# A gated attention and token-mixer kernel: o visits in twos and ones, and one ring of six banks for s and ms

## The chip, the cores and the metric

The kernel runs on one core of a Trainium2 chip. The time is the device time of the program in microseconds (us). Before the change it was 1692.79 us, the median of three runs (1692.36 to 1693.18). A profile of one further execution shows what each engine does: PE is TensorE's matmuls, PEld its weight loads, DVE VectorE, ACT ScalarE, POOL GpSimd, and SP the queue that issues the DMAs.

## The reference

With S = 2048 rows, D = 640 columns, H = 32 query heads of 20 columns, one key head and one value head, and F = 1728:

```python
g = sigmoid((x * gate_w).sum(-1, keepdims=True))
q = heads(A_x @ A_wq)                      # 32 heads of 20
k, v = A_x @ A_wk, A_x @ A_wv              # one head each
p = softmax(q k^T * 20 ** -0.5)
a = join(p @ v) @ A_wo
h = layernorm(B_x)
u = gelu(h^T @ B_w1 + B_b1)                # along the rows
b = (u @ B_w2 + B_b2)^T
out = g * a + (1 - g) * b
```

All inputs are fp32. The kernel splits operands in a high and a low part (`_hi`, `_lo`) and adds three products (high by high, low by high, high by low), so most matmuls come in threes.

## The kernel before

An opening part projects q, k and v, writes q to memory (`q_scr`), and computes a first share of the mixer. Then comes the loop that this case is about.

**Units.** Attention is cut in 32 groups of (four heads by 512 query columns), and each group in 16 blocks of 128 keys: 512 units `(n, kb)` in all. A unit has these steps:

- `qk` (L642): four matmuls named s, one for each head, on half of TensorE's rows (head half `b`, rows 0 to 63 or 64 to 127). An s fills one PSUM bank of 512 columns. ScalarE's exp (L652) turns it to a tile p in SBUF.
- `pv_mm` (L670): the o visit. Four heads' p by v, on four column tiles of 32, added up over the 16 units of a group in one bank o. At the group's last unit o is read by VectorE (transpose L685), scaled, transposed back (L692), split and stored to `o_scr`; these steps stand in `later` and are taken one or two at a time by `settle` (L972).
- `ms_next` (L454): the maxima that the softmax subtracts. An ms is a matmul of 128 queries by 512 keys on one row half, and VectorE's reduce (L469) reads it. 64 of them make a group's maxima. `ms_done` (L476) reduces them to `mm` (L480, VectorE) and makes `mn` of it in three GpSimd operations (L482 to L484). `store_max` (L487) transposes `mn` on VectorE (L490) and stores it, at the visit of unit 7 of the group before; `fetch_max` (L493), at that of unit 9, loads the maxima as extra rows of q.

**Fillers.** The rest of TensorE's work in the loop is cut in matmuls of 64 rows by 320 columns that all add into one bank, g: the remaining 18 tiles of the mixer's first product (`b1_jobs`, 96 fillers each), its second product (`b2_jobs`, 32 parts of 81), and a part of the output projection (`a_job`, 30 fillers for 128 rows by 320 columns). When fillers pass from one row half to the other, `signal` (L660) puts a small VectorE operation (`flag`) between them.

**The loop.** 488 stretches, each followed by one visit. In stretch `k`, row half `b = k % 2` has four s and three or four ms (`lane_x`), the other half has some ten fillers and one ms or none (`lane_f`); `beside` (L947) writes the two lanes in one order by the estimates `X_US` and `F_US`. Half `b` makes its s of units `k - 1` and `k`. Then follows the visit of unit `k - 1`. In `batches` (L903) a part of the first product is cut in 5 x 2 stretches and one of the second in 4 x 2; a part of the output projection takes 3 (`a_job`).

**The tail.** The last 24 visits have no ms left. `stretch` (L1011) makes one visit once, and then two at a time, over s and the rest of the output projection (`tail_job`, `tail_take`). A closing part adds the last four heads and stores eight pieces.

**Banks.** Of eight PSUM banks, three are `ps_m` (ms), three `ps_s` (s), one g and one o. Tiles p rotate through 12 buffers.

**What the output projection loads.** `load_o` and `load_y` bring o and y back for a tile; `wo2` and the last two columns of `oTs` hold copies of two chunks at the other row half, so that a part's fillers can be parted unevenly between the halves.

Of the kernel before, what the change touches and what calls it, by code (L numbers as in the profile page):

```python
# [17 lines left out]
P = 128  # L18
# [6 lines left out]
NB = 512  # L25
# [5 lines left out]
TAIL = 24  # L31
EPS = 1e-5
# [5 lines left out]
def mix_kernel(ctx: ExitStack, tc: tile.TileContext, A_x, A_wq, A_wk, A_wv, A_wo,  # L38
# [411 lines left out]
    mtiles = {}  # L450
    given = [0, 0]
    issued = [0, 0]

    def ms_next(b):  # L454
# [7 lines left out]
        def step():  # L462
            if n not in mtiles:
                mtiles[n] = mpool.tile([P, 16, 4], F32, name="mp")
            ms = ps_m.tile([P, NB], F32, name="ms")
            nc.tensor.matmul(ms, qmax[n][64 * b:64 * b + 60, pr, qt * P:(qt + 1) * P],  # L466
                             kst[64 * b:64 * b + 60, kq * NB:(kq + 1) * NB], start=True, stop=True)
            c = (2 * b + pr) * 4 + qt
            nc.vector.tensor_reduce(mtiles[n][:, c, kq:kq + 1], ms, axis=AX.X, op=ALU.max)  # L469
            issued[b] += 1  # L470
            if min(issued) == 32 * n + 1:
                new_qmax(n + 1)
# [82 lines left out]
    with tc.tile_pool(name="psb", bufs=2, space=PSUM, side="right") as psb:  # L555
# [8 lines left out]
        for fc in range(PRO):  # L564
# [32 lines left out]
    OC = DC + 2  # L597
    oTs = [slot[1][:, 2 * DC * D + i * 2 * OC * P:2 * DC * D + (i + 1) * 2 * OC * P]
           .rearrange("p (j c q) -> p j c q", j=2, q=P) for i in range(2)]
    twin = ctx.enter_context(tc.tile_pool(name="twin", bufs=1))  # L600
    wo2 = [twin.tile([P, 2, HD2], F32R, name=name) for name in ("wo2_hi", "wo2_lo")]
    yts = []
    pools = {}

    def second():
        right.close()
        ys = ctx.enter_context(tc.tile_pool(name="ys", bufs=1, side="right"))
        yts.extend(ys.tile([P, D], F32, name=f"y{i}") for i in range(2))
        pools["rows"] = ctx.enter_context(tc.tile_pool(name="rows", bufs=3, side="right"))
# [12 lines left out]
    def load_wo2():  # L622
        wos[DC] = fin.tile([P, D], F32, name="yo")
        for d in range(2):
            o = 64 * (1 - d)
            nc.sync.dma_start(out=wos[DC][o:o + 64, :].rearrange("p (c e) -> p c e", c=2),
                              in_=A_wo[:2 * P, d * HD2:(d + 1) * HD2].rearrange("(c h p) e -> h p c e", c=2, h=2)[d])

    def split_wo2():
        wr = wos[DC].rearrange("p (c e) -> p c e", c=2)  # L630
        nc.gpsimd.tensor_copy(wo2[0], wr)
        nc.gpsimd.tensor_sub(wo2[1], wr, f32(wo2[0]))

# [6 lines left out]
    odd_s = [0]  # L640

    def qk(u, pr, b):  # L642
# [4 lines left out]
        odd_s[0] ^= 1  # L647
        s = ps_m.tile([P, NB], F32, name="ms") if spare[0] and odd_s[0] and not loaded else ps_s.tile([P, NB], F32, name="s")
        nc.tensor.matmul(s, kst[64 * b:64 * b + 62, kb * P:(kb + 1) * P], q[64 * b:64 * b + 62, pr, :],  # L649
                         start=True, stop=True)  # L650
        p = pp_pool.tile([P, NB], F32, name="p")
# [89 lines left out]
    def load_o(st):  # L741
        cols = slice(st * P, (st + 1) * P)
        for j in range(2):
            oT = f32(oTs[st % 2][:, j])
            nc.sync.dma_start(out=oT[:, :DC], in_=o_scr[j, :, cols].rearrange("(c p) s -> p c s", p=P))
            for h in range(2):
                nc.sync.dma_start(out=oT[64 * (1 - h):64 * (2 - h), DC:],
                                  in_=o_scr[j, :2 * P, cols].rearrange("(c h p) s -> h p c s", c=2, h=2)[h])

    def load_y(st):  # L750
        nc.sync.dma_start(out=yts[st % 2], in_=y_scr[st * P:(st + 1) * P, :])
# [6 lines left out]
    NA = NS - 7  # L758
    jobs = [(st, 0, D) for st in range(NS - 8, NS - 4)]
# [3 lines left out]
    def room(i):  # L763
        t, at = (u0, 3 * D * i) if i < 4 else (slot[0], 3 * D * (i % 4))
# [55 lines left out]
    def a_job(st, d):  # L820
        hold = {}
        sl = slice(d * HD2, (d + 1) * HD2)
        last_one = st == NA - 1

        def mm(c, k, half):
            if not hold:
                hold["p"], hold["n"] = ps_g.tile([P, NB], F32, name="g"), 0
            hold["n"] += 1
            r = slice(64 * half, 64 * half + 64)
            o = oTs[st % 2][r, k % 2, c, :]  # L830
            w = (wo_lo if k == 2 else wo_hi)[r, c, sl] if c < DC else wo2[k // 2][r, c - DC, :]
            other_tile(half, nc.tensor.matmul(hold["p"][:, :HD2], o, w,  # L832
                                              start=(hold["n"] == 1), stop=(hold["n"] == 6 * DC)))

        def done():
            if d == 0:
                rows_a[st] = fin.tile([P, D], F32, name="yo")
            at = rows_a[st]
            nc.scalar.activation(at[:, sl], hold["p"][:, :HD2], AF.Copy, scale=g_col[:, st:st + 1])
            nc.gpsimd.tensor_add(at[:, sl], at[:, sl], yts[st % 2][:, sl])  # L840
            if d == 1 or last_one:
# [3 lines left out]
        def steps(half, cks):  # L845
            return [lambda c=c, k=k: mm(c, k, half) for c, k in cks]

        every = [(c, k) for c in range(OC) for k in range(3)]
        if last_one:
            own = every[:3 * DC]  # L850
            fs = [steps(1, own[:8]), steps(0, own[:8]), steps(1, own[8:]), steps(0, own[8:])]
        else:
            most, few = every[:-1], every[5:3 * DC]
            fs = [steps(1 - d, most[:10]), steps(d, few), steps(1 - d, most[10:])]
        out = [(f, [], []) for f in fs]
        out[-1][2].append(done)
        if d == 0 and not last_one:
            out[0][1].extend((lambda: load_o(st + 1), lambda: load_y(st + 1)))
        return out

    rows_a = {}
# [55 lines left out]
    k_tail = len(units) - TAIL  # L917
    todo = [divmod(i, FC) for i in range(PRO, 2 * FC)]
    seq = batches([b1_jobs(*t) for t in todo], [5] * len(todo))
    for i, (steps, rest, done) in enumerate(seq):  # L920
        item, j = divmod(i + 1, 5)
        rest.insert(0, lambda c=4 * (PRO + item) + (48 * j // 5) // 12: w1_upto(c + 4))
    b2 = [b2_jobs(st) for st in range(NS)]
    m = len(seq)
    seq += batches(b2, [4] * 2 * NS)
    for st in range(NS - 1):
        for j, n in ((1, 1), (2, 2), (3, 4)):
            seq[m + 8 * st + 4 + j][1].append(lambda c=W2 + 4 * (st + 1) + n: w1_upto(c))
# [4 lines left out]
    seq[m + 9 + 8 * DC][1].append(load_wo2)  # L933
    seq[m + 11 + 8 * DC][1].append(split_wo2)
    seq[-8][1].append(lambda: load_o(0))
    seq[-1][1].append(lambda: load_y(0))
    ph = [(rows[1 - b], rest if b else [], done if b else []) for rows, rest, done in seq for b in range(2)]
    for st in range(NA):
        for d in range(2 if st < NA - 1 else 1):
            ph += a_job(st, d)  # L940
    assert len(ph) == k_tail
    for i, k in enumerate((443, 451, 459, 467, 473, 477, 481, 485)):
        ph[k][1].append(lambda i=i: tail_load(i))

    X_US, F_US = 0.232, 0.147

    def beside(rows0, rows64, x):  # L947
        lanes = [list(rows0), list(rows64)]
        at = [0.0, 0.0]
        while lanes[0] or lanes[1]:  # L950
            k = 0 if lanes[0] and (not lanes[1] or at[0] <= at[1]) else 1
            if k == x and len(lanes[k]) == 1 and lanes[1 - k]:
                k = 1 - k
            us, f = lanes[k].pop(0)
            f()
            at[k] += us

    def lane_x(ss, ms):
        out = []
        for x in ss:  # L960
            out += [(X_US, y) for y in ms[:1]] + [(X_US, x)]
            ms = ms[1:]
        return out + [(X_US, y) for y in ms]

    def lane_f(ms, fs, end):
        return [(F_US, f) for f in fs] + [(0.0, f) for f in [signal] + end] + [(X_US, y) for y in ms]
# [5 lines left out]
    def settle(k):  # L972
# [14 lines left out]
    for k in range(k_tail):  # L987
        b = k % 2
        ss = [lambda u=u, pr=pr: qk(u, pr, b) for u in (k - 1, k) for pr in range(2) if u >= 0]
        fs, rest, done = ph[k]  # L990
        ms = [[f for f in (ms_next(x) for _ in range(c)) if f] for x, c in (((b, 3), (1 - b, 1)) if len(fs) < 12 else ((b, 4), (1 - b, 0)))]
        lanes = [None, None]
        lanes[b] = lane_x(ss, ms[0])
        lanes[1 - b] = lane_f(ms[1], fs, done)
        if k == 0:
            (m0, m1, m2), (s0, s1) = ms[0], ss
            lanes[0] = [(3 * X_US, m0), (3 * X_US, m1), (X_US, s0), (X_US, m2), (X_US, s1)]
        beside(*lanes, b)
# [5 lines left out]
        if k == k_tail - 4:  # L1004
            raw = last_wo()
        if k == k_tail - 2:
            w_last = split_last(raw)
        if k:
            visit(k - 1)

    def stretch(k, n):  # L1011
        lanes = [None, None]
        for b in range(2):
            own = [j for j in range(k, k + n) if j % 2 == b]
            ss = [lambda u=u, pr=pr, b=b: qk(u, pr, b) for j in own for u in (j - 1, j) for pr in range(2) if u < len(units)]
            fs = tail_take(b, math.ceil(len(tail[b]) * n / (len(units) + 1 - k)) + (n == 1) * (3 if not ss else -3))
            cut = [0] + [round(len(fs) * x) for x in ((0.25, 0.5, 0.75, 1.0) if n == 1 else
                                                          (0.18, 0.53, 0.82, 1.0) if b == k % 2 else (0.41, 0.71, 1.0, 1.0))]
# [67 lines left out]
```

## Time and profile before

| | us |
|---|---|
| median of three runs | 1692.79 |
| the profiled execution, its own time | 1692.96 |
| its span, from the first to the last instruction | 1691.2 |

The granted TensorE clock is 1.000 over the whole span. The page gives busy times as unions over each engine, so a lane beside another is not counted twice. A row of a group names its line, engine, operation, tiles and shapes, its count, its busy time, the mean length of one in ns, and the idle time ahead of it with what ended it. In rows in order of time the first number is the start and the second how long the merged instructions took; a matmul's length contains its passage through the array, so its neighbour in the same lane starts earlier than it ends.

### The profile page before, as it was taken

How to read it: one execution, taken by the hardware profiler on the slowest of the kernel's cores; microseconds unless marked ns; L12 is line 12 of the kernel's file. 1: busy time of each engine (PE TensorE's matmuls, PEld its weight loads, DVE VectorE, ACT ScalarE, POOL GpSimd, SP SyncE). 2: the span in 40 equal slices, each digit the busy share in tenths (PEclk: the TensorE clock that was granted, in tenths of full speed). 3: DMA queues.
4: the chain of work that ended last, by engine and by line, in shares of the span. 5: the costliest groups of instructions: out<-in, count | busy, mean ns of one | idle time of the engine just before them, and what ended most of it. 6: DMA issues, size and time to landing. Idle time of an engine off the chain costs nothing.

```text
span 1691.2 us, 39115 instructions
## 1 busy us (share of the span) xinstructions
PE 1683.8 (100%) x14865; PEld 1100.5 (65%) x14865; DVE 1433.7 (85%) x2913; ACT 1186.7 (70%) x2323; POOL 574.0 (34%) x726
## 2 busy tenths in 40 slices
PE   9999999999999999999999999999999999999998
PEld 7899766666666666666666666666666666666666
DVE  6679888888888888888888888888888888888834
ACT  4444677777777777777777777777777777777775
POOL 6467644543545454322222222222211122111200
PEclk9999999999999999999999999999999999999999
DMA  7665322222222222112122222121112222455511
GB/s 209 196 178 148 95 64 64 65 64 68 59 71 71 71 64 70 54 54 55 44 70 70 68 71 63 57 61 52 50 36 63 62 60 66 103 159 157 153 57 50
DMA packets 180450, 139.13 MB, mean 82 GB/s; under 512 B 33402, under 2 KB 146455, under 8 KB 180263
## 3 DMA queue, kind: packets, MB, share of 16 engines
q1 hardware_dynamic: 180262, 136.63, 29.2%
q8 instruction: 117, 1.92, 0.5%
q14 instruction: 71, 0.57, 0.1%
HBM read 103.94 MB, written 31.65 MB: 80 GB/s over the span
## 4 chain that ended last, share of the span: by engine, by line
PE 96%; issue 2%; DVE 1%; DMA 0%; ACT 0%; POOL 0%; SPq 0%; POOLq 0%; DVEq 0%; ACTq 0%
PE o L676 30%; PE s L649 18%; PE ms L466 17%; PE g L721 12%; PE g L894 8%; PE pu L576 4%; PE pp L293 4%; PE g L832 2%; PE ms L794 1%; PE pt L285 0%; PE pp L357 0%; DMA xb<-in_A_x_dram 0%; DVE mp L469 0%; PE g L794 0%; PE pp L182 0%
## 5 line engine op out<-in xcount | busy, mean ns | idle before, releaser
L469 DVE TENSOR_REDUCE mp<-ms 128x1 f32<-128x512 f32 x2048 | 1278.5, 684 | 166.6 <-PE ms L466 160.5
L652 ACT ACTIVATE p<-s 128x512 f32<-128x512 f32 x2048 | 1067.1, 604 | 393.8 <-PE s L649 389.2
L466 PE MATMUL ms<-kst,qmx 60*128 60x512 f32 x2048 | 848.5, 419 | 0.5 <-DVE mp L469 0.4
L649 PE MATMUL s<-qst,kst 62*128 62x512 f32 x2048 | 744.3, 404 | 0.0
L676 PE MATMUL o<-p,v_sb 128*32 128x512 f32 x4096 | 555.3, 604 | 0.0
L466 PEld LDWEIGHTS ms<-kst,qmx 60*128 60x128 f32 x2048 | 378.3, 185 | 207.3 <-DVE flag L662 181.1
L649 PEld LDWEIGHTS s<-qst,kst 62*128 62x128 f32 x2048 | 379.0, 186 | 13.3 <-issue 10.9
L894 PE MATMUL g<-slot,wh 64*128 64x320 f32 x1152 | 281.4, 318 | 0.0
L124 POOL TENSOR_TENSOR wl<-wr,wh 128x512 fp32r<-128x512 f32 (+1 forms) x176 | 220.5, 1255 | 35.1 <-ACT wh L121 22.6
L123 POOL CAST wh<-wr 128x512 fp32r<-128x512 f32 (+1 forms) x136 | 79.8, 587 | 443.1 <-PE g L721 280.0
L894 PEld LDWEIGHTS g<-slot,wh 64*128 64x128 f32 x1152 | 190.6, 184 | 59.9 <-DVE flag L662 59.9
L721 PE MATMUL g<-u,wh 64*128 64x320 f32 x864 | 208.8, 317 | 0.0
L721 PE MATMUL g<-slot,wh 64*128 64x320 f32 x864 | 208.8, 317 | 0.0
L676 PEld LDWEIGHTS o<-p,v_sb 128*32 128x32 f32 x4096 | 94.2, 108 | 137.6 <-issue 130.3
L894 PE MATMUL g<-slot,wl 64*128 64x320 f32 x576 | 179.4, 311 | 0.0
L721 PEld LDWEIGHTS g<-slot,wh 64*128 64x128 f32 x864 | 142.4, 184 | 40.2 <-DVE flag L662 40.2
L721 PEld LDWEIGHTS g<-u,wh 64*128 64x128 f32 x864 | 142.4, 184 | 40.2 <-DVE flag L662 40.2
L721 PE MATMUL g<-slot,wl 64*128 64x320 f32 x432 | 135.1, 313 | 0.0
L721 PE MATMUL g<-u,wl 64*128 64x320 f32 x432 | 134.9, 313 | 0.0
L894 PEld LDWEIGHTS g<-slot,wl 64*128 64x128 f32 x576 | 106.1, 184 | 15.1 <-DVE flag L662 15.1
L721 PEld LDWEIGHTS g<-slot,wl 64*128 64x128 f32 x432 | 79.6, 184 | 13.4 <-DVE flag L662 13.4
L721 PEld LDWEIGHTS g<-u,wl 64*128 64x128 f32 x432 | 79.5, 184 | 13.4 <-DVE flag L662 13.4
(201 smaller groups left out, 1417.8 us busy)
## 6 DMA issues: line engine op xcount, KB each, us to landing
wr<-in_B_w_dram SPq DMA_DIRECT2D x152, 256.0 KB
qmx<-q_scr SPq DMA_DIRECT2D x192, 80.0 KB
qst<-q_scr SPq DMA_DIRECT2D x192, 80.0 KB
slot<-o_scr SPq DMA_DIRECT2D x18, 320.0 KB
y_scr<-yo SPq DMA_DIRECT2D x16, 320.0 KB
o_scr<-oh SPq DMA_DIRECT2D x124, 40.0 KB
o_scr<-ol SPq DMA_DIRECT2D x124, 40.0 KB
q_scr<-qh SPq DMA_DIRECT2D x19, 256.0 KB
```

The source lines that it names most:

```text
L123: nc.gpsimd.tensor_copy(wh, wr)
L124: nc.gpsimd.tensor_sub(wl, wr, f32(wh))
L293: nc.tensor.matmul(pp, w, t, start=first and n == 0, stop=not more and n == len(steps) - 1)
L466: nc.tensor.matmul(ms, qmax[n][64 * b:64 * b + 60, pr, qt * P:(qt + 1) * P], kst[64 * b:64 * b + 60, kq * NB:(kq + 1) * NB], start=True, s ...
L469: nc.vector.tensor_reduce(mtiles[n][:, c, kq:kq + 1], ms, axis=AX.X, op=ALU.max)
L576: nc.tensor.matmul(pu[r][:, :HD2], w[rows, c, :], h[rows, st, :], start=(st == 0 and k == 0), stop=(st == NS - 1 and k == 2))
L649: nc.tensor.matmul(s, kst[64 * b:64 * b + 62, kb * P:(kb + 1) * P], q[64 * b:64 * b + 62, pr, :], start=True, stop=True)
L652: nc.scalar.activation(p, s, AF.Exp, scale=SCALE)
L676: nc.tensor.matmul(o[32 * hh:32 * hh + 32, :], v_sb[:, kb, :], ptiles.pop((u, hh)), start=(kb == 0), stop=(kb == NS - 1), skip_group_check ...
L721: other_tile(half, nc.tensor.matmul(hold["p"][:, :HD2], w[r, fc % HS, :], u[d][r, fc, :], start=(hold["n"] == 1), stop=(hold["n"] == 6 * F ...
L832: other_tile(half, nc.tensor.matmul(hold["p"][:, :HD2], o, w, start=(hold["n"] == 1), stop=(hold["n"] == 6 * DC)))
L894: other_tile(half, nc.tensor.matmul(hold["p"][:, :HD2], w[r, st % HS, :], h[d][r, st, :], start=(hold["n"] == 1), stop=(hold["n"] == 6 * NS)))
```

## The change

- The loop goes over 326 stretches: none, two, one, two, one ... visits behind them. Parts of the first product are cut in 3 x 2 stretches (16 fillers each), of the second in 3 x 2 (13 or 14), of the output projection in 2 (15).
- A stretch has six s on half `b`. With 16 fillers it has five ms there and one on the other half; with fewer, five and two before two visits, four and one before one visit. The orders are written out in `MANY` and `FEW`, and `merged` lays the lanes side by side. The s are no longer tied to `k`: `s_next` gives each half its next s.
- Where two visits stand together and the first is the last of its group, it goes to the middle of the stretch.
- `next_bank` takes `ps_m` and `ps_s` in turn for s and ms alike. Two more p buffers are used once the maxima are done.
- The tail has blocks of three and two visits (`BLOCKS`).
- The output projection in the loop ends at half of tile 6 instead of half of tile 8; the tail has the more. The copies `wo2` and the two further columns of `oTs` go.
- At the end, the stores are issued after the computation, six on SP's queue and two on ScalarE's.

```diff
+BLOCKS = (3, 3, 2, 3, 3, 3, 3, 2, 2)
...
+    ring = []
+
+    def next_bank():
+        if not ring:
+            return ps_m.tile([P, NB], F32, name="ms")
+        ring[0] ^= 1
+        return ps_m.tile([P, NB], F32, name="ms") if ring[0] else ps_s.tile([P, NB], F32, name="s")
...
-            ms = ps_m.tile([P, NB], F32, name="ms")
+            ms = next_bank()
...
+    def next_p():
+        turn_p[0] += spare[0]
+        i = turn_p[0] % 14
+        return extra_p[i - 1] if 0 < i < 3 else pp_pool.tile([P, NB], F32, name="p")
+
+    def s_next(b):
+        j = sc[b]
+        if j >= 2 * len(units):
+            return None
+        sc[b] += 1
+        return lambda: qk(j // 2, j % 2, b)
...
-        s = ps_m.tile([P, NB], F32, name="ms") if spare[0] and odd_s[0] and not loaded else ps_s.tile([P, NB], F32, name="s")
+        s = ps_s.tile([P, NB], F32, name="s") if spare[0] else next_bank()
...
-    NA = NS - 7
-    jobs = [(st, 0, D) for st in range(NS - 8, NS - 4)]
+    NA = NS - 9
+    jobs = [(st, 0, D) for st in range(NA - 1, NS - 4)]
...
-    seq = batches([b1_jobs(*t) for t in todo], [5] * len(todo))
+    seq = batches([b1_jobs(*t) for t in todo], [3] * len(todo))
...
-    seq += batches(b2, [4] * 2 * NS)
+    seq += batches(b2, [3] * 2 * NS)
...
+    seq += batches(aj, [1] * (2 * NA - 1))
...
-    for k in range(k_tail):
-        b = k % 2
-        ss = [lambda u=u, pr=pr: qk(u, pr, b) for u in (k - 1, k) for pr in range(2) if u >= 0]
+    FEW = (("smsssmssmmm", "mFm"), ("smsmsmssms", "Fm"))
+    MANY = (("msmsmsssmsm", "Fm"), ("msmsmsssmsm", "Fm"))
+
+    def main(k, vs):
+        b = k % 2
         fs, rest, done = ph[k]
...
+            sx, sf = (MANY if len(fs) > 15 else FEW)[len(vs) == 1]
+            lx = [(X_US, (s_next if c == "s" else ms_next)(b)) for c in sx]
+            lf = []
+            for c in sf:
+                lf += fill if c == "F" else [(X_US, (s_next if c == "s" else ms_next)(1 - b))]
+        order = merged(lx, lf)
+        for i, f in enumerate(order):
+            if len(vs) == 2 and 2 * i >= len(order):
+                settle()
+                if units[vs[0]][1] == NS - 1:
+                    visit(vs[0])
+                vs = vs[1:] if units[vs[0]][1] == NS - 1 else vs + [None]
+            f()
         ms_done()
         spare[0] = len(row_max) == NU
-        settle(k)
+        settle()
         for f in rest:
             f()
...
+        for v in vs:
+            if v is not None:
+                visit(v)
...
+    for k in range(len(ph)):
+        n = 0 if k == 0 else 1 + k % 2
+        main(k, list(range(v, v + n)))
+        v += n
...
+    for n in BLOCKS:
+        ends = [min(2 * len(units), 2 * (v + n) + (1 if n == 3 else 2)) for _ in range(2)]
...
+        for _ in range(n):
+            settle()
+            visit(v)
+            v += 1
...
-            nc.sync.dma_start(out=y_out[st * P:(st + 1) * P, sl], in_=at[:, :HD2])
+            ends[i, d] = at
+    for q, order in ((nc.sync, ((0, 0), (1, 0), (0, 1), (2, 1), (1, 1), (2, 0))), (nc.scalar, ((3, 0), (3, 1)))):
+        for i, d in order:
+            st = NS - 4 + i
+            q.dma_start(out=y_out[st * P:(st + 1) * P, d * HD2:(d + 1) * HD2], in_=ends[i, d][:, :HD2])
```

More of the change, by code (lines that the diff above doesn't have):

```diff
@@ L596, in mix_kernel @@
     wo_hi, wo_lo = (slot[1][:, i * DC * D:(i + 1) * DC * D].rearrange("p (c d) -> p c d", d=D) for i in range(2))
[L597 to L603, printed above, removed]
+    oTs = [slot[1][:, 2 * DC * D + i * 2 * D:2 * DC * D + (i + 1) * 2 * D].rearrange("p (j c q) -> p j c q", j=2, q=P)
+           for i in range(2)]
+    yts = [f32(slot[1][:, 2 * DC * D + 4 * D + i * D:2 * DC * D + 4 * D + (i + 1) * D]) for i in range(2)]
+    pools, extra_p = {}, []
     def second():
         right.close()
-        ys = ctx.enter_context(tc.tile_pool(name="ys", bufs=1, side="right"))
-        yts.extend(ys.tile([P, D], F32, name=f"y{i}") for i in range(2))
+        xp = ctx.enter_context(tc.tile_pool(name="xp", bufs=1, side="right"))
+        extra_p.extend(xp.tile([P, NB], F32, name=f"p{i}") for i in range(2))
         pools["rows"] = ctx.enter_context(tc.tile_pool(name="rows", bufs=3, side="right"))
@@ L620, in split_wo @@
         nc.gpsimd.tensor_sub(wo_lo[:, c, :], wr, f32(wo_hi[:, c, :]))
[L622 to L632, printed above, removed]
     units = [(n, kb) for n in range(NU) for kb in range(NS)]
@@ L818, in tail_take, with a_jobs, load, mm @@
         return out
-    def a_job(st, d):
+    def a_jobs(st):
         hold = {}
[L822 to L826, printed above, removed]
+        ds = (0,) if st == NA - 1 else (0, 1)
+        def load():
+            oT, yt = oTs[st % 2], yts[st % 2]
+            load_a(st, D, oT, yt)
+            hold["o"], hold["y"] = oT, yt
+        total = 6 * DC
+        def mm(c, k, d, half):
+            if not hold.get("n"):
                 hold["p"], hold["n"] = ps_g.tile([P, NB], F32, name="g"), 0
+            oT = hold["o"]
+            o, w = ((oT[:, 0], wo_hi), (oT[:, 1], wo_hi), (oT[:, 0], wo_lo))[k]
@@ L828, in mm @@
             hold["n"] += 1
             r = slice(64 * half, 64 * half + 64)
[L830 to L835, printed above, removed]
-            if d == 0:
[L837 to L841, printed above, removed]
+            other_tile(half, nc.tensor.matmul(hold["p"][:, :HD2], o[r, c, :], w[r, c, d * HD2:(d + 1) * HD2],
+                             start=(hold["n"] == 1), stop=(hold["n"] == total)))
@@ new lines, in done @@
+        def done(d):
+            sl = slice(d * HD2, (d + 1) * HD2)
+            if d == 0:
+                hold["a"] = fin.tile([P, D], F32, name="yo")
+            at, yt = hold["a"], hold["y"]
+            hold["n"] = 0
+            if spare[0]:
+                nc.vector.scalar_tensor_tensor(at[:, sl], hold["p"][:, :HD2], g_col[:, st:st + 1], yt[:, sl],
+                                               op0=ALU.mult, op1=ALU.add)
+            else:
+                nc.scalar.activation(at[:, sl], hold["p"][:, :HD2], AF.Copy, scale=g_col[:, st:st + 1])
+                nc.gpsimd.tensor_add(at[:, sl], at[:, sl], yt[:, sl])
+            if d == ds[-1]:
@@ L842, in done @@
                 e = slice(0, (d + 1) * HD2)
                 nc.sync.dma_start(out=y_out[st * P:(st + 1) * P, e], in_=at[:, e])
[L845 to L861, printed above, removed]
+        return load, [([[lambda h=h, c=c, k=k, d=d: mm(c, k, d, h) for h in range(2)]
+                        for c in range(DC) for k in range(3)],
+                       lambda d=d: done(d)) for d in ds]
     def spare_row(i, dt=F32):
@@ L1007, in mix_kernel @@
             w_last = split_last(raw)
[L1008 to L1018, printed above, removed]
-            lanes[b] = [x for i in range(4) for x in [(X_US, y) for y in ss[i:i + 1]] +
-                        [(F_US, f) for f in fs[cut[i]:cut[i + 1]]]]
-        beside(*lanes, None)
-        for j in range(k, k + n):
-            settle(j)
-            if 13 <= j - k_tail < 17:
-                tail_load(8 + j - k_tail - 13)
-            visit(j - 1)
@@ L1028, in mix_kernel @@
-    stretch(k_tail, 1)
-    for k in range(k_tail + 1, len(units), 2):
-        stretch(k, 2)
+    assert v == len(units) - TAIL and spare[0]
+    for n in BLOCKS:
+        ends = [min(2 * len(units), 2 * (v + n) + (1 if n == 3 else 2)) for _ in range(2)]
+        lanes = [[], []]
+        own = [(2 * len(units) - c) * X_US for c in sc]
+        i = 0
+        while any(sc[b] < ends[b] for b in range(2)):
+            b = int(sc[1] < sc[0])
+            lanes[b].append((max(0.0, 0.55 + (i - 2) * EXP_US) if i > 2 else 0.0, s_next(b)))
+            i += 1
+        left = len(units) - v
+        fs = [tail_take(b, len(tail[b]) if n == left else
+                        max(0, round(((own[b] + len(tail[b]) * F_US) * n / left - len(lanes[b]) * X_US) / F_US)))
+              for b in range(2)]
+        at = [0.0, 0.0]
+        while any(lanes) or any(fs):
+            b = 0 if at[0] <= at[1] and (lanes[0] or fs[0]) or not (lanes[1] or fs[1]) else 1
+            if lanes[b] and (lanes[b][0][0] <= at[b] or not fs[b]):
+                lanes[b].pop(0)[1]()
+                at[b] += X_US
+            else:
+                fs[b].pop(0)()
+                at[b] += F_US
+        for _ in range(n):
+            settle()
+            visit(v)
+            v += 1
+        waiting = {j for h in range(2) for j, _ in tail[h]}
+        while len(loaded) < len(jobs) and len(loaded) - 8 not in waiting and (len(loaded) < 10 or v >= 501):
+            tail_load(len(loaded))
@@ L1047, in mix_kernel @@
     oh, ol = osplit
+    ends = {}
     for i in range(4):
```

91 lines of the change are left out of this document (37 added, 54 removed).

## The prediction

> **What bounds the kernel now.** I read the page first (busy times, chain of waits, costliest groups), then busy time by stage, then the order of time on the engines. The page's shares:
>
> ```profile
> span 1691.2 us, 39115 instructions
> ...
> PE 1683.8 (100%) x14865; PEld 1100.5 (65%) x14865; DVE 1433.7 (85%) x2913; ACT 1186.7 (70%) x2323; POOL 574.0 (34%) x726
> ...
> PE 96%; issue 2%; DVE 1%; DMA 0%; ACT 0%; POOL 0%; SPq 0%; POOLq 0%; DVEq 0%; ACTq 0%
> PE o L676 30%; PE s L649 18%; PE ms L466 17%; PE g L721 12%; PE g L894 8%; PE pu L576 4%; PE pp L293 4%; PE g L832 2%; PE ms L794 1%; PE pt L285 0%; PE pp L357 0%; DMA xb<-in_A_x_dram 0%; DVE mp L469 0%; PE g L794 0%; PE pp L182 0%
> ...
> L469 DVE TENSOR_REDUCE mp<-ms 128x1 f32<-128x512 f32 x2048 | 1278.5, 684 | 166.6 <-PE ms L466 160.5
> L652 ACT ACTIVATE p<-s 128x512 f32<-128x512 f32 x2048 | 1067.1, 604 | 393.8 <-PE s L649 389.2
> ```
>
> TensorE is the chain, and nothing it waits for is large. VectorE is next at 85%. Busy time by stage (first fillers, second fillers, output fillers, tail, end; columns are stretch and length, then PE, PEld, DVE, ACT, POOL):
>
> ```profile
> 179.50:703.00 523.50, 523.39 (x4596) 326.62 (x4597) 466.04 (x953) 390.56 (x771) 245.50 (x321) 1.00 0.25 67
> 703.00:1455.50 752.50, 752.50 (x6692) 469.47 (x6692) 665.87 (x1361) 546.97 (x1060) 175.64 (x236) 1.00 0.21 58
> 1455.50:1607.70 152.20, 152.20 (x1346) 94.35 (x1342) 134.95 (x277) 114.65 (x226) 29.35 (x39) 1.00 0.60 161
> 1607.70:1678.60 70.90, 70.90 (x697) 45.68 (x695) 23.84 (x47) 50.81 (x101) 3.43 (x6) 1.00 0.14 41
> ```
>
> The loop's 180 + 256 + 52 stretches take 2.908, 2.939 and 2.927 us, 1428.2 in all. Inside one, TensorE in order of time:
>
> ```profile
> 1004.91 0.40 PE L466 MATMUL ms<-kst,qmx 60*128 60x512 f32 x1
> 1005.23 1.06 PE L676 MATMUL o<-p,v_sb 128*32 128x512 f32 x8
> 1006.23 0.42 PE L721 MATMUL g<-u,wh 64*128 64x320 f32 x1
> 1006.23 0.50 PE L466 MATMUL ms<-kst,qmx 60*128 60x512 f32 x1
> 1006.49 0.31 PE L721 MATMUL g<-u,wh 64*128 64x320 f32 x1
> 1006.57 0.39 PE L649 MATMUL s<-qst,kst 62*128 62x512 f32 x1
> ...
> 1007.74 0.47 PE L649 MATMUL s<-qst,kst 62*128 62x512 f32 x1
> 1007.81 0.30 PE L721 MATMUL g<-u,wl 64*128 64x320 f32 x1
> ```
>
> Two lanes run side by side. An s or ms follows another after 0.234 (five steps from 1006.57 to 1007.74), a filler after 0.147 (nine steps from 1006.49 to 1007.81). The first step after a visit is longer: 0.34 and 0.26. From the last start to the visit is 0.32; from visit to the next row start 1.00. The tail already has two visits in a row:
>
> ```profile
> 1615.49 1.92 PE L676 MATMUL o<-p,v_sb 128*32 128x512 f32 x16
> 1617.35 0.50 PE L649 MATMUL s<-qst,kst 62*128 62x512 f32 x2
> ```
>
> That is 1.86, so the second costs 0.86. One turn from row tiles to column tiles and back therefore costs (0.34 - 0.234) + (0.32 - 0.234) + (1.00 - 0.86) = 0.33 us.
>
> My formula for a stretch is: last start of the longer lane, + 0.32, + the visit. Seven entries end at 0.34 + 5 x 0.234 = 1.51; 9.6 fillers, then ms, at 0.26 + 8.6 x 0.147 = 1.52. Stage one gets 2.84 (measured 2.908); stage two, with 10.1 fillers, 2.92 (2.939). I add 0.04 a stretch.
>
> **The change: fewer turns.** 488 stretches become 326, with the same matmuls in them and in the tail. Pairs of stretches (two visits, one visit):
>
> - Stage one, 54 pairs, eleven entries against sixteen fillers and an ms: 0.34 + 9 x 0.234 = 2.45 and 0.26 + 15 x 0.147 = 2.465. Pair: 2 x (2.465 + 0.32 + 0.04) + 1.00 + 1.86 = 8.51; total 459.5.
> - Stage two, 96 pairs, some 13.5 fillers. One visit: ten entries, 2.21, with 0.36 behind them 2.57. Two visits: eleven entries, 2.45 without waits.
> - Output stage, 13 pairs, 15 fillers. One visit: 0.26 + 14 x 0.147 = 2.32, so 2.68. Two visits: at most 2.54 in the filler lane.
>
> **The ring.** Six banks alternate whatever they hold, so each allocation waits for the one six before it. The rows that price it:
>
> ```profile
> 1003.34 0.49 PE L466 MATMUL ms<-kst,qmx 60*128 60x512 f32 x1
> 1003.67 0.39 PE L649 MATMUL s<-qst,kst 62*128 62x512 f32 x1
> 1003.87 2.50 DVE L469 TENSOR_REDUCE mp<-ms 128x1 f32<-128x512 f32 x4 [0.44 <-PE ms L466]
> 1004.10 2.06 ACT L652 ACTIVATE p<-s 128x512 f32<-128x512 f32 x4 [0.81 <-PE s L649]
> ...
> 602.64 1.25 DVE L469 TENSOR_REDUCE mp<-ms 128x1 f32<-128x512 f32 x2
> 603.35 0.49 PE L466 MATMUL ms<-kst,qmx 60*128 60x512 f32 x1
> ```
>
> A reduce starts 0.53 after a first ms, then each 0.605 ((2.50 - 0.684) / 3). An exp starts 0.43 after its s (0.54 after a first one, whose matmul is 0.11 longer), then each 0.485. A bank is taken again 0.03 after the reader's mean end (602.64 + 0.684 to 603.35); I use 0.05.
>
> Stage one, order m s m s m s s s m s m m: the tenth taker needs the second s's bank (0.77 + 0.485 + 0.65 = 1.91, wanted at 2.21), the eleventh the third reduce's (0.53 + 1.21 + 0.73 = 2.47, wanted at 2.45). It fits. Stage two with two visits, s m m s s s m s s m m m m: the ninth needs the second reduce's bank, 0.53 + 0.605 + 0.73 = 1.87 against 1.74; the twelfth the fourth s's, 0.54 + 3 x 0.485 + 0.65 = 2.65 against 2.45. So that lane ends at 2.65 and the stretch is 2.65 + 0.36 = 3.01. Pair: 2.57 + 3.01 + 2.86 = 8.44, total 810.2 (791 without the wait, the lower end). Output pairs: 2.68 + 3.01 + 2.86 = 8.55, total 111.2.
>
> 459.5 + 810.2 + 111.2 - 1.3 (the opening stretch has no visit) = 1379.6: **-48.6**.
>
> **Visits in mid-stretch.** Where a unit's last visit is the first of two, it goes to the middle: every third unit, 10 times, an added turn of 0.33 and uneven lane ends, 0.4 together: **+4** (3 to 8).
>
> **VectorE's lumps.** The row maximum's last step:
>
> ```profile
> 997.62 0.22 DVE L480 TENSOR_REDUCE mm<-mp 128x16 f32<-128x64 f32 x1
> 997.93 0.25 POOL L482 TENSOR_SCALAR mm<-mm 128x16 f32<-128x16 f32 x1 [8.78 <-DVE mm L480]
> 998.03 2.50 DVE L469 TENSOR_REDUCE mp<-ms 128x1 f32<-128x512 f32 x4 [0.18 <-PE ms L466]
> ...
> 998.53 0.22 POOL L484 TENSOR_TENSOR mn<-mm,mn 128x16 fp32r<-128x16 f32 x1
> ...
> 1000.44 0.20 DVE L490 STREAM_TRANSPOSE mt<-mn 128x32 f32<-128x32 f32 x1
> ...
> 603.49 1.28 POOL L124 TENSOR_TENSOR wl<-wr,wh 128x512 fp32r<-128x512 f32 x1
> ```
>
> Before, four reduces lie between `mm` and `mt`, and hide GpSimd's three operations (1.13 us from 997.62 to 998.75). In the changed instruction order `mt` stands right behind `mm` in all 31 units. VectorE then stands still until GpSimd is done, some 1.2 us, 1.4 with the transpose, longer if GpSimd is in an operation like the 1.28 above. All reduces queue behind it, then the ring, then TensorE. The other lumps are as before, two transposes a unit:
>
> ```profile
> L685 DVE STREAM_TRANSPOSE ot<-o 128x512 f32<-128x512 f32 x32 | 22.9, 717 | 4.1 <-PE o L676 4.0
> L692 DVE STREAM_TRANSPOSE on<-ot 128x512 f32<-128x512 f32 x32 | 22.5, 702 | 0.1
> ```
>
> VectorE's free time was 2.91 - 4 x 0.605 = 0.49 a stretch. Now, in stage one, it is 3.83 - 3.63 = 0.20 or 4.69 - 3.63 = 1.06; in stage two 4.87 - 4.24 = 0.63 or 3.57 - 3.03 = 0.54. A 1.4 lump overruns by 0.3 to 1.2, a 0.7 lump by 0 to 0.5. Bounds a unit: 0 (the ring absorbs it) to 1.4 + 2 x 0.7 = 2.8; I take 0.8, nearer the overruns than the ends: 30 x 0.8 = **+24** (0 to 84).
>
> VectorE has 7.26 of reduces in 8.5 us, 85%, so it stays under TensorE on average. The Trainium skill ("TensorEngine Tiling (Array Packing)", PSUM Bottleneck) warns that tiling speeds up TensorE and not PSUM evacuation, which may then become the bottleneck. Here that speaks against the change; by that rule alone the +24 would stand nearer its upper end, by the rows it does not.
>
> SP's queue moves too: `mt` is stored at a unit's visit 7 and fetched at visit 9, but the next unit's first s now stands behind visit 13, not 14: 4 x 2.83 = 11 us for what took 14.6. SP's longest wait between store and fetch is short beside that, so this costs nothing; without that room the s themselves would wait.
>
> ```profile
> SPq L498 <- DMA m_scr<-mt: 33.9, 27, 3.2
> ```
>
> **Tail and end.** Fillers and s of the tail before:
>
> ```profile
> 1607.70:1678.60 70.90, 41.62 (x390) 37.97 (x390) 1.00 0.14 41
> 1607.70:1678.60 70.90, 37.05 (x98) 15.84 (x98) 1.00 0.14 41
> ```
>
> Output tile 7 and a half each of tiles 6 and 8 move there: 120 fillers more (510), 60 a lane x 0.147 = +8.8; 13 groups of visits become 9: -1.3; five s fewer, -0.6: **+7**. The last stores:
>
> ```profile
> 1685.79 3.07 SPq L1064 DMA_DIRECT2D out_dram<-p  x6
> ...
> 1686.47 0.54 DVE L1059 SCALAR_TENSOR_TENSOR p<-ms,g_col,row 128x320 f32<-128x320 f32 x1
> ```
>
> SP issues one after another until 1688.86; the last result is ready at 1687.01. Two go to ScalarE's queue, so issuing ends near 1687.5: **-1** (-1.3 to 0). Loads of `wo2` and `oT` fall away from an SP that TensorE does not wait for: nothing, and if that cover were gone a load's microseconds at the stage's start.
>
> **Sum.** The profiled execution's own time is 1692.96, 0.17 over the median. 1692.96 - 48.6 + 4 + 24 + 7 - 1 = 1678.4, so **1678** on the median's scale.
>
> **Rivals.**
>
> 1. *VectorE's lumps reach TensorE whole; slower.* Place: the `mm` to `mt` stand and the transposes. Without the lumps the sum is -38.6, so it decides from 38.6 / 30 = 1.29 us a unit. At 2.8, and GpSimd's 1.28 ahead of a third of the stands, 3.2 x 30 = 96: 1692.96 - 38.6 + 96 = 1750. For it: 0.20 free in stage one. Against: the longer stretch beside it has 1.06. Near 1.29 lies no change, 1690 to 1696.
> 2. *Both waits hide.* Ring and lumps cost nothing: 1692.96 - 48.6 - 20.7 + 4 + 7 - 1 = 1634; lumps alone hidden: 1654. Against: the twelfth taker's bank is late in every such stretch by the rows' own spacing.
> 3. *The second visit is not cheap in the loop,* because exps of its p come late; it saves 0.14 less plus a wait. 0.2 x 163 = 33: 1711 at worst. Against: a double visit needs only the stretch's third s; in stage one that starts at 1.28, its exp ends by 2.4, and the visit starts at 2.79.
>
> **Chances.** Forecast (1662 to 1689) 0.72; rival 1 slower 0.09, its no-change band 0.06; rival 2 0.10; rival 3 0.03. No change is within 0.2%, 3.4 us. Faster 0.83, same 0.06, slower 0.11. The range takes the lumps from 0.3 to 1.3 a unit and the ring from half to all: 1662 to 1694.
>
> **What would show it.** Right: 325 groups of visits in the loop, 10 more from mid-stretch ones; 0.86 for a second visit; stage-one pairs near 8.5; stage-two pairs near 8.44 with an ms late behind an exp; VectorE idle about 0.9 before each `mt`, put down to GpSimd's `mn`, and a long stretch there. The stage with ms and fillers ends near 1587, the tail takes 78. Wrong: pairs above 8.9 outside unit ends, VectorE idle over 2 us at `mt`, or exps that hold visits.

## The result, and the profile after

| | before | after |
|---|---|---|
| median, us | 1692.8 | 1702.62 (1702.29 to 1703.20) |
| ratio to before | | 1.0058 (95% interval 1.0041 to 1.0076) |
| profiled execution, us | 1692.96 | 1702.31 |
| its span, us | 1691.2 | 1700.5 |

The changed kernel is slower, by about 0.6%; 1678 was forecast, and 1662 to 1694 as the range. The page of the changed kernel (span, busy times, chain, costliest groups):

```profile
span 1700.5 us, 38944 instructions
...
PE 1686.0 (99%) x14865; PEld 1100.1 (65%) x14865; DVE 1439.9 (85%) x2759; ACT 1176.9 (69%) x2319; POOL 568.8 (33%) x720
...
PE 92%; DVE 4%; issue 2%; POOL 1%; DMA 0%; ACT 0%; POOLq 0%; ACTq 0%
...
L477 DVE TENSOR_REDUCE mp<-ms 128x1 f32<-128x512 f32 x1081 | 706.2, 683 | 95.0 <-PE ms L474 82.0
...
L477 DVE TENSOR_REDUCE mp<-s 128x1 f32<-128x512 f32 x967 | 633.4, 683 | 39.7 <-PE s L474 39.4
```

The matmuls are as many as before. VectorE has gone from 1% to 4% of the chain. In the ring either kind of step may stand in a bank called `ms` or `s`, so from here on the line tells the kind: L474 is an `ms` step, L654 an `s` step; the `o` line is L681. Busy time by stage of the changed kernel (first fillers, second fillers, output fillers, tail; columns as in the prediction):

```profile
179.30:655.50 476.20, 473.66 (x4306) 304.83 (x4307) 420.56 (x799) 351.45 (x700) 241.81 (x314) 1.00 0.27 69
655.50:1497.00 841.50, 837.12 (x7206) 503.77 (x7207) 746.46 (x1435) 609.46 (x1189) 180.91 (x246) 1.00 0.20 55
1497.00:1610.50 113.50, 112.77 (x1013) 71.92 (x1009) 101.41 (x195) 85.44 (x170) 23.29 (x30) 1.00 0.59 167
1610.50:1688.20 77.70, 77.36 (x807) 54.82 (x799) 27.82 (x55) 46.73 (x94) 3.40 (x6) 1.00 0.20 60
```

The three stages of the loop take 1431.2 together, against 1428.2 before and 1407.6 in the prediction's sum (1379.6 + 4 + 24); the tail takes 77.7 against 70.9. So nearly the whole miss lies in the loop. Visits in order of time, TensorE of the changed kernel, four in stage one and four in stage two:

```profile
288.22 1.06 PE L681 MATMUL o<-p,v_sb 128*32 128x512 f32 x8
292.12 1.92 PE L681 MATMUL o<-p,v_sb 128*32 128x512 f32 x16
296.88 1.07 PE L681 MATMUL o<-p,v_sb 128*32 128x512 f32 x8
300.78 1.92 PE L681 MATMUL o<-p,v_sb 128*32 128x512 f32 x16
...
799.14 1.07 PE L681 MATMUL o<-p,v_sb 128*32 128x512 f32 x8
803.28 1.92 PE L681 MATMUL o<-p,v_sb 128*32 128x512 f32 x16
807.76 1.06 PE L681 MATMUL o<-p,v_sb 128*32 128x512 f32 x8
811.90 1.92 PE L681 MATMUL o<-p,v_sb 128*32 128x512 f32 x16
```

A pair of stretches is 3.90 + 4.76 = 8.66 in stage one (forecast 8.51) and 4.14 + 4.48 = 8.62 in stage two (8.44); these are also the medians over each stage, and output pairs are 8.62 as well (8.55). That is 54 x 0.15 + 96 x 0.18 + 13 x 0.07 = 26 us in undisturbed pairs, where the whole loop is 1431.2 - 1407.6 = 24 above the forecast.

Where in a pair? TensorE and then its weight loads (PEld) at the end of the stretch before 292.12:

```profile
291.43 0.39 PE L654 MATMUL s<-qst,kst 62*128 62x512 f32 x1
291.52 0.30 PE L895 MATMUL g<-slot,wh 64*128 64x320 f32 x1
291.69 0.49 PE L474 MATMUL ms<-kst,qmx 60*128 60x512 f32 x1
291.69 0.49 PE L474 MATMUL s<-kst,qmx 60*128 60x512 f32 x1
292.12 0.64 PE L681 MATMUL o<-p,v_sb 128*32 128x512 f32 x4
```

```profile
291.20 0.19 PEld L654 LDWEIGHTS s<-qst,kst 62*128 62x128 f32 x1
...
291.69 0.18 PEld L474 LDWEIGHTS ms<-kst,qmx 60*128 60x128 f32 x1
291.69 0.18 PEld L474 LDWEIGHTS s<-kst,qmx 60*128 60x128 f32 x1
```

The `s` at 291.43 has its weights loaded from 291.20 on, 0.23 ahead, and takes 0.39. The two last `ms` begin to load at 291.69 and to multiply at 291.69, and take 0.49. The visit starts when they are nearly through: 292.12 - 291.69 = 0.43 after the last start, where the prediction had 0.32. The medians in stage one and stage two are 0.42 to 0.43; in the output stage it is 0.39 before two visits and 0.32 before one. The same place in the kernel before, the stretch that the prediction shows (visit at 1005.23), weight loads:

```profile
1004.75 0.18 PEld L649 LDWEIGHTS s<-qst,kst 62*128 62x128 f32 x1
1004.76 0.18 PEld L466 LDWEIGHTS ms<-kst,qmx 60*128 60x128 f32 x1
```

There the last `ms` loads at 1004.76, 0.15 ahead of its start at 1004.91, and takes 0.40. Both kernels let the visit begin some 0.07 before the last row matmul ends; the difference is how long that matmul is. (The profile models where a matmul ends; the 0.43 and the 0.32 are taken between two starts and do not rest on that.)

What is late is the bank. VectorE and ScalarE of the changed kernel, the same stretch:

```profile
289.75 3.16 DVE L477 TENSOR_REDUCE mp<-ms 128x1 f32<-128x512 f32 x5
```

```profile
289.98 1.58 ACT L657 ACTIVATE p<-s 128x512 f32<-128x512 f32 x3 [0.86 <-PE s L654]
```

Of the two last `ms`, the eleventh taker of a bank needs that of the third reduce, and the twelfth that of the third exp, which ends at 289.98 + 1.58 = 291.56. The third reduce by itself:

```profile
290.95 0.68 DVE L477 TENSOR_REDUCE mp<-ms 128x1 f32<-128x512 f32 x1
```

It ends at 291.63, and the load that needs its bank, and that the profile has waiting for it, starts at 291.69. The prediction had this bank in time for the *matmul* (2.47 where 2.45 was wanted) and stopped there. The wait stands on the weight load ahead of it.

The other thing to see is the stand at `mt`. The row of `mt` with its idle time, from the view of the tile `mt`, and VectorE in order of time at one of them:

```profile
  POOL mn L492: 29.4, 31
```

```profile
957.94 0.22 DVE L488 TENSOR_REDUCE mm<-mp 128x16 f32<-128x64 f32 x1
959.11 0.21 DVE L498 STREAM_TRANSPOSE mt<-mn 128x32 f32<-128x32 f32 x1 [0.95 <-POOL mn L492]
```

```profile
959.95 0.49 PE L654 MATMUL ms<-qst,kst 62*128 62x512 f32 x1 [0.54 <-DVE mp L477]
```

The last row is TensorE: its row lane waits for a reduce, and that stretch lasts 5.00 (visits at 956.67 and 961.67) in place of 4.14.

### The profile page after: what moved, and what is told of

Same layout as the page of the kernel before. It is cut to its first block, busy times and chain, and to the rows that moved or that the text cites. A ratio compares the mean times of both kernels' runs of the same rounds, so it can differ in the third digit from the quotient of the medians.

```text
span 1700.5 us, 38944 instructions
## 1 busy us (share of the span) xinstructions
PE 1686.0 (99%) x14865; PEld 1100.1 (65%) x14865; DVE 1439.9 (85%) x2759; ACT 1176.9 (69%) x2319; POOL 568.8 (33%) x720
## 4 chain that ended last, share of the span: by engine, by line
PE 92%; DVE 4%; issue 2%; POOL 1%; DMA 0%; ACT 0%; POOLq 0%; ACTq 0%
PE o L681 27%; PE ms L474 11%; PE s L654 11%; PE g L726 9%; PE ms L654 8%; PE s L474 7%; PE g L895 6%; PE pp L294 4%; PE pu L584 3%; DVE mp L477 3%; PE g L841 1%; PE ms L797 1%; PE pt L286 0%; PE pp L358 0%; PE g L797 0%
## 5 line engine op out<-in xcount | busy, mean ns | idle before, releaser
L477 DVE TENSOR_REDUCE mp<-ms 128x1 f32<-128x512 f32 x1081 | 706.2, 683 | 95.0 <-PE ms L474 82.0
L657 ACT ACTIVATE p<-s 128x512 f32<-128x512 f32 x1079 | 610.3, 615 | 214.8 <-PE s L654 145.4
L657 ACT ACTIVATE p<-ms 128x512 f32<-128x512 f32 x969 | 543.3, 608 | 195.0 <-PE ms L654 159.2
L477 DVE TENSOR_REDUCE mp<-s 128x1 f32<-128x512 f32 x967 | 633.4, 683 | 39.7 <-PE s L474 39.4
L681 PE MATMUL o<-p,v_sb 128*32 128x512 f32 x4096 | 510.7, 600 | 0.0
L474 PE MATMUL ms<-kst,qmx 60*128 60x512 f32 x1081 | 458.5, 434 | 0.4 <-DVE mp L477 0.4
L654 PE MATMUL s<-qst,kst 62*128 62x512 f32 x1079 | 445.3, 418 | 1.3
L654 PE MATMUL ms<-qst,kst 62*128 62x512 f32 x969 | 404.4, 417 | 6.0 <-DVE mp L477 6.0
L474 PE MATMUL s<-kst,qmx 60*128 60x512 f32 x967 | 400.0, 430 | 0.4 <-DVE yo L520 0.4
L654 PEld LDWEIGHTS s<-qst,kst 62*128 62x128 f32 x1079 | 197.9, 185 | 128.3 <-DVE flag L667 90.5
L474 PEld LDWEIGHTS ms<-kst,qmx 60*128 60x128 f32 x1081 | 198.1, 184 | 124.0 <-ACT p L657 63.7
L654 PEld LDWEIGHTS ms<-qst,kst 62*128 62x128 f32 x969 | 179.6, 185 | 108.9 <-issue 67.1
L681 PEld LDWEIGHTS o<-p,v_sb 128*32 128x32 f32 x4096 | 97.8, 108 | 186.2 <-issue 180.8
L474 PEld LDWEIGHTS s<-kst,qmx 60*128 60x128 f32 x967 | 179.0, 185 | 17.5 <-DVE mp L477 14.6
```

Of the source, the lines that this page charges most:

```text
L657: nc.scalar.activation(p, s, AF.Exp, scale=SCALE)
L681: nc.tensor.matmul(o[32 * hh:32 * hh + 32, :], v_sb[:, kb, :], ptiles.pop((u, hh)), start=(kb == 0), stop=(kb == NS - 1), skip_group_check ...
```

## The experiments

In these texts theory L is the one of the late bank and the uncovered weight load; rival T says that the longer gap belongs to alternating two visits with one, whoever empties the banks. The stand alone in the kernel before and the half exps ran on a chip on which the kernel before took 1693.07 (median), the other four kernels on one on which it took 1693.41.

**The ring alone, in the kernel before.**

```diff
-            ms = ps_m.tile([P, NB], F32, name="ms")
+            ms = next_bank()
...
+    ring.append(0)
```

The `s` up to the last unit's maxima take `next_bank()` too.

> The kernel before with the one ring of six banks alone (s and ms in turn), nothing else changed. Theory L: eight takers a stretch, each bank free well before it is wanted; the gap to the visit stays at 0.33 and the time within 0.2% of before (1690 to 1696). Rival R (a ring shared by two readers costs by itself, since one late reader holds the other's matmuls): gap 0.42 or stretches of 3.0 us and more, 1705 or slower.

Measured: 1692.84, ratio 0.9997 (0.9987 to 1.0007). Stretches stay at 2.90 and 2.94 and the last start stands 0.33 ahead of the visit. Rival R falls: the ring costs nothing where a stretch takes eight banks or so, and what is late in the changed kernel comes with the longer stretch. The changed kernel with three banks each for s and ms was not run.

**The stand at `mt` taken away, in the changed kernel.** The store of the row maximum, with its `mt`, goes from a unit's visit 7 to visit 9, and the fetch from 9 to 10.

```diff
-        if kb == 7 and n + 1 < NU:
-            store_max(n + 1)
         if kb == 9 and n + 1 < NU:
+            store_max(n + 1)
+        if kb == 10 and n + 1 < NU:
             fetch_max(n + 1)
```

> The changed kernel with the maxima's transpose and store at the visit of unit 9 and their fetch at unit 10 (before: 7 and 9), so that reduces lie between mm and mt. Theory L (a late bank holds the last weight load ahead of each visit, and the VectorE stand at mt is a second, smaller cost): the stand of 0.95 us at each of 31 mt goes, the long stretches there lose 0.3 to 0.9 us each, some 18 us in all: 1685 us (1680 to 1691); the start of the last row matmul to the visit stays at 0.42 us, and the pairs stay at 8.66 (stage one) and 8.62 (stage two). Rival D (VectorE's stand is the whole miss of 25 us): 1678 or less, and pairs unchanged only if the miss was never in them. Rival N (the stand is hidden): 1702.

Measured: 1685.53 (1685.18 to 1685.93), ratio to before 0.9953 (0.9938 to 0.9968), faster than both kernels; rivals D and N fall. VectorE at one unit, in order of time:

```profile
949.07 0.22 DVE L488 TENSOR_REDUCE mm<-mp 128x16 f32<-128x64 f32 x1
953.88 0.20 DVE L498 STREAM_TRANSPOSE mt<-mn 128x32 f32<-128x32 f32 x1
```

`mt` comes 4.8 after `mm` here, and no idle time stands before it; VectorE's reduces are 0% of the chain again. The stages end at 650.0, 1480.5 and 1593.5:

```profile
179.30:650.00 470.70, 470.34 (x4302) 304.39 (x4304) 420.75 (x800) 351.01 (x701) 240.65 (x313) 1.00 0.27 70
650.00:1480.50 830.50, 830.02 (x7204) 503.08 (x7200) 746.60 (x1434) 606.04 (x1188) 180.91 (x245) 1.00 0.20 56
1480.50:1593.50 113.00, 112.34 (x1013) 71.94 (x1016) 101.72 (x196) 85.43 (x171) 23.30 (x30) 1.00 0.59 167
```

The loop is 1414.2, so the stands cost 17.0, 0.55 each. Steady pairs are unchanged (3.90 and 4.76; 4.14 and 4.48), and so is the 0.42: the stand is one cost, the gap another.

**The stand alone, in the kernel before.** The store goes from visit 7 to visit 6, so that `mt` follows `mm` at once.

```diff
-        if kb == 7 and n + 1 < NU:
+        if kb == 6 and n + 1 < NU:
             store_max(n + 1)
```

> The kernel before, with the store of the row maximum (and mt) one visit earlier, so that mt stands directly behind mm on VectorE in 31 units, as in the changed kernel; nothing else differs. Theory (the stand is a price of that place alone, whatever the order of the loop): VectorE idles 0.95 before each mt, put down to GpSimd's mn, and a stretch of the old order has 0.49 of free VectorE time, so each stand costs 0.3 to 0.8 us: 1702 to 1718. Rival A (the old order absorbs it, the stand matters only where six banks are taken twice in a stretch): 1692 to 1696. Rival B (the lump reaches TensorE whole, 1.15 x 31): 1728 or more.

Measured: 1713.14 (1713.02 to 1713.40), ratio 1.0119 (1.0102 to 1.0136): +20.1, or 0.65 a stand. The view of the tile `mt`, and one stand on VectorE:

```profile
  POOL mn L484: 29.9, 31
```

```profile
913.48 0.22 DVE L480 TENSOR_REDUCE mm<-mp 128x16 f32<-128x64 f32 x1
914.65 0.21 DVE L490 STREAM_TRANSPOSE mt<-mn 128x32 f32<-128x32 f32 x1 [0.95 <-POOL mn L484]
```

The price belongs to the place, and the old order pays it as the new one does: rival A falls, and rival B too, since about 0.5 of the 1.15 from `mm` to the end of `mt` is absorbed.

**Half of each reduce left out**, in the changed kernel (256 of 512 columns; the exps are whole).

```diff
-            nc.vector.tensor_reduce(mtiles[n][:, c, kq:kq + 1], ms, axis=AX.X, op=ALU.max)
+            nc.vector.tensor_reduce(mtiles[n][:, c, kq:kq + 1], ms[:, :NB // 2], axis=AX.X, op=ALU.max)
```

> The changed kernel with each ms reduced over 256 of its 512 columns: half of the maximum is left out. Theory L: in stage one no ms waits for a bank, the weight loads of the last two ms run ahead, the last matmul starts where it did (2.48 us into the stretch) but the visit follows 0.33 us later and not 0.42; a pair falls from 8.66 to 8.45 to 8.50. In stage two the twelfth bank taker still waits for the fourth exp, so the stretch with two visits behind it keeps 0.42. Time 1660 to 1672 with the lumps gone too. Rival T (a turn from row to column tiles takes 0.42 in long stretches, or where both lanes end together, whatever the banks do): 0.42 stays in stage one, a pair stays above 8.6, time above 1672.

Measured: 1671.41 (one run). Stage one: pairs of 3.84 + 4.67 = 8.51, the gap 0.38 before two visits and 0.36 before one, by the medians. Stage two: as in the changed kernel, 4.14 and 4.48 with 0.42. TensorE and its loads at a visit of stage one (287.84):

```profile
287.48 0.43 PE L474 MATMUL s<-kst,qmx 60*128 60x512 f32 x1
287.84 1.92 PE L681 MATMUL o<-p,v_sb 128*32 128x512 f32 x16
```

```profile
287.42 0.18 PEld L474 LDWEIGHTS s<-kst,qmx 60*128 60x128 f32 x1
```

The load comes 0.06 ahead, the matmul takes 0.43, the gap is 0.36. The gap moves with the reader of the bank, which refutes T in stage one. It does not fall to the 0.33 that L had put there: the exps, still whole, are next in line (the profile has this load waiting for an exp). In stage two they hold the banks by themselves.

**Half of each exp left out**, in the changed kernel (the visits read the half twice; the reduces are whole).

```diff
-        nc.scalar.activation(p, s, AF.Exp, scale=SCALE)
+        nc.scalar.activation(p[:, :NB // 2], s[:, :NB // 2], AF.Exp, scale=SCALE)
```

> The changed kernel with half of each exp left out (256 of 512 columns, the visits read the half twice); the reduces stay whole. Theory L (a bank that comes free less than a lane's step before it is taken leaves the weight load of the last matmul uncovered): stage one, where reduces hold the last bank, stays at 3.90 and 4.76 with 0.42 from the last start to the visit; in stage two the row part of the two-visit stretch falls from 2.72 to about 2.45 and the 0.42 falls towards 0.33 where exps alone hold the bank, so 3.75 to 3.9 and 4.36 to 4.48; in all 1655 to 1685. Rival T (0.42 belongs to alternating two visits and one): 0.42 in both stages, only the 0.27 of the row part goes: 96 x 0.27 = 26, so 1676. Rival M (VectorE alone sets both stages once the exps are short): pairs of 8.6 as before in both stages, 1695 to 1703.

Measured: 1685.26 (one run), just above the 1655 to 1685 that was expected; rival M falls. Stage one stays at 3.90 and 4.76 with 0.425. In stage two the gap falls to 0.32 and 0.33 (pairs 4.03 + 4.40 = 8.43). TensorE and its loads at the visit at 804.90:

```profile
804.52 0.45 PE L474 MATMUL s<-kst,qmx 60*128 60x512 f32 x1
804.57 0.40 PE L654 MATMUL ms<-qst,kst 62*128 62x512 f32 x1
804.90 1.06 PE L681 MATMUL o<-p,v_sb 128*32 128x512 f32 x8
```

```profile
804.47 0.18 PEld L474 LDWEIGHTS s<-kst,qmx 60*128 60x128 f32 x1
804.48 0.18 PEld L654 LDWEIGHTS ms<-qst,kst 62*128 62x128 f32 x1
```

A load 0.05 ahead gives 0.45, one 0.09 ahead gives 0.40, and the visit follows 0.33 after the last start. T falls in stage two as well. One expectation of L fails: the row part of the two-visit stretch does not go to 2.45, it stays at 2.71, and so the pair's first part is 4.03 and not 3.75 to 3.9.

**Both halves left out.**

> As the run with half reduces, and each exp over 256 of its 512 columns too; the o visit reads the half that is there twice, so its matmuls keep their size. Left out: half of the maxima and half of the exps. Theory L: no bank is late anywhere, last start to visit 0.33 in all stages, pairs 8.45 (one) and 8.15 to 8.25 (two), time 1625 to 1640. Rival T: 0.42 stays in all stages, 326 x 0.09 = 29 us more, 1655 to 1670.

Measured: 1612.72 (one run), below the 1625 to 1640 that was expected. Pairs are 3.77 + 4.63 = 8.40 and 3.75 + 4.36 = 8.11, the gap 0.32 in every stage, the row part of stage two's two-visit stretch 2.43. Weight loads and matmuls at a visit of stage one (303.06):

```profile
302.49 0.19 PEld L474 LDWEIGHTS ms<-kst,qmx 60*128 60x128 f32 x1
302.59 0.18 PEld L474 LDWEIGHTS s<-kst,qmx 60*128 60x128 f32 x1
```

```profile
302.73 0.39 PE L474 MATMUL ms<-kst,qmx 60*128 60x512 f32 x1
302.73 0.40 PE L474 MATMUL s<-kst,qmx 60*128 60x512 f32 x1
303.06 1.92 PE L681 MATMUL o<-p,v_sb 128*32 128x512 f32 x16
```

It is the same order of instructions, with two visits and one in turn. With the banks back in time the loads come 0.24 and 0.14 ahead and the gap is the old 0.33. So the 0.42 is the banks' doing wherever it stands. The row part of 2.71 takes either reader to hold it: reduces whole 2.71, exps whole 2.72, neither 2.43.

The span falls by 1700.5 - 1610.9 = 89.6. Steady pairs give 54 x 0.26 + 96 x 0.51 + 13 x 0.29 = 67 of it; the rest, 23, is near what lies outside steady pairs in the changed kernel's loop without its mid-stretch visits (25.3 - 2.9 below), though some 2 of it stand behind the loop. Shorter pairs than expected (54 x 0.05 + 96 x 0.09 = 11, from 8.45 and 8.20) are part of the 12 to 27 by which the expectation was too high; what it took for the lumps it does not say.

## Why the prediction was wrong, by its own steps

The measured sum beside the forecast one, on the profiled execution's 1692.96:

| step | forecast | measured | from |
|---|---|---|---|
| fewer turns, with the ring | -48.6 | -22.3 | steady pairs: 54 x 8.66 + 96 x 8.62 + 13 x 8.62 - 1.3 = 1405.9, less 1428.2 |
| mid-stretch visits | +4 | +2.9 | 2.66 + 2.36 + 3.89 = 8.91 for two stretches of 8.62, x 10 |
| VectorE's lumps | +24 | +22.4 | loop 1431.2 - 1405.9 = 25.3, less 2.9 |
| tail | +7 | +6.8 | 77.7 - 70.9 |
| end | -1 | -0.3 | 12.6 (1678.6 to 1691.2) to 12.3 (1688.2 to 1700.5) |

The sum is 1702.5; the execution took 1702.31.

*The turns and the second visit: right.* A single visit takes 1.00 and a double one 1.85 in the loop, as in the tail before; rival 3 has no support. The row starts of stage one were right too (2.48 for 2.465), and those of stage two before one visit (2.21 for 2.21).

*The step that failed: "+ 0.32", from the last start to the visit, taken over from the kernel before into each stretch of the new one.* It is 0.42 in stage one and stage two. The 0.04 that the prediction added a stretch covers some of it; the other 0.06, in the 2 x (54 + 96) stretches of their pairs, makes 18 of the 26 missed. Most of the remaining 8 is the twelfth taker of the two-visit stretch in stage two, 2.72 for 2.65 (96 x 0.07 = 7): there the prediction had the wait right, and its size a little short. The constant 0.32 looked like a property of the change of tiles. It is the length of the last row matmul less 0.07, and that length depends on whether its weights could be loaded ahead, which depends on when its bank comes back. The ring paragraph had the bank's time in stage one right to 0.01 (2.47; the load starts at 2.48) and asked whether it delays the matmul's start. It should have asked whether it delays the load, which needs about 0.1 more. In the kernel before, a stretch takes about eight banks out of six and the load is 0.15 ahead; with twelve or so out of six the last banks are those taken in the middle of the same stretch, and no slack is left. The prediction's own lines held the sign: the first `ms` behind a visit (1006.23), whose load starts with it, takes 0.50, and the one at 1004.91 takes 0.40.

The prediction's sign of being wrong in the pairs was 8.9; pairs of 8.66 and 8.62 lie below it, and 0.16 in each of 163 pairs was enough. The lower end of its range does not come out of its own terms either: lumps at 0.3 and the ring at half give 1678.4 - 15 - 10 = 1653, not 1662.

*The lumps: right in size, and the larger part shown.* The 0.8 a unit was a choice between bounds of 0 and 2.8, so that it came so near is partly luck. The 31 stands cost 17.0, by taking them away, 0.55 each. The transposes have what remains of 22.4, 5.4, by subtraction alone. The idle time before `mt` is 0.95, put down to GpSimd's `mn`, as forecast. Rival 1 puts the point of decision at 1.29 a unit; measured was 22.4 / 30 = 0.75. So the kernel came out slower with the lumps near their forecast, not through rival 1: the gain that they were set against was half as large.

*The rule on evacuation.* VectorE is busy for 85% of the span, before and after, and by the rows its lumps stayed near the forecast. But the two readers of the banks, VectorE and ScalarE, do bound the loop: with half their work left out the same matmuls end 89.6 sooner, of which 67 in the steady pairs. The Trainium skill ("TensorEngine Tiling (Array Packing)", PSUM Bottleneck) warns that evacuation may become the bottleneck; this run agrees. The prediction looked for it in VectorE's share, in the lumps and in the one bank that it had late for its matmul, and the larger part of what it missed was in banks that are late for a load alone.

*The tail was right; the end was half right.* SP's six stores and ScalarE's two rows at the end of the changed kernel, and VectorE's last result:

```profile
1693.62 3.50 SPq L1084 DMA_DIRECT2D out_dram<-p  x6
```

```profile
1696.29 0.89 ACTq L1084 DMA_DIRECT2D out_dram<-p  x2
```

```profile
1696.17 0.54 DVE L1075 SCALAR_TENSOR_TENSOR p<-ms,g_col,row 128x320 f32<-128x320 f32 x1
```

Issuing ends at 1697.18, 0.47 after the last result (1696.71), where it was 1.85 after it before (1688.86 and 1687.01). That is the gain that the prediction saw. But from the last issue to the end of the span it now takes 3.3 us, not 2.3, and most is given back. No run took this apart.

*Which way to go.* With `mt` away from `mm` the change is a gain, 1685.53. The 0.42 remains in it: an order without late returns would be worth 2 x (54 + 96) x 0.09 = 27 us by the gap alone, as an estimate from these rows. None was run.

## What to carry to other kernels

In these traces a matmul's wait for its PSUM bank holds its weight load back as well, so count a bank's return against the load and not against the matmul: a bank that is in time for the start by less than about 0.1 us still makes the matmul longer (0.49 for 0.39 at worst), and the visit behind it waits for that. A constant read off one schedule (here 0.32 from the last start to the visit) is to be taken apart into what makes it up before it is carried into a schedule that uses the banks harder. And keep instructions that wait for another engine's answer away from the one that puts the question: the same 0.95 us stand cost 0.55 in the new order and 0.65 in the old, and was gone from the trace once `mt` stood two visits later.

## What the runs showed of the hardware

The length of a 128x512 row-tile matmul follows how far ahead its weight load starts: 0 ahead 0.49, 0.05 ahead 0.45, 0.06 ahead 0.43, 0.09 ahead 0.40, 0.14 to 0.24 ahead 0.39 to 0.40. The load itself is 0.18 to 0.19 long in each of these rows, so only about half of it shows when nothing covers it. Over all 4096 s and ms of the changed kernel the median length is 0.496 where the load starts less than 0.01 ahead (1129 of them) and 0.392 where it starts 0.20 to 0.25 ahead (2431).

A bank is loaded for again some 0.05 after the end of its reduce (291.63 to 291.69), which is what the prediction allowed. A stand of 0.95 on VectorE, followed by a transpose, costs TensorE only 0.55 to 0.65, though VectorE is busy for 85% of the span; what takes up the rest was not taken apart.
